# A planned kernel whose planner holds late work out of the opening and counts transposes behind a full wire as longer

## The chip, the cores and the metric

The kernel runs on one core of one Trainium2 chip. The metric is the device time of one execution in microseconds (us).

Engines are named as in the profile: PE is the tensor engine, PEld its weight loads, DVE the vector engine, ACT the scalar engine, POOL the GpSimd engine, SP the queue that issues the loads and the transposes. PSUM is the memory that the matmul results are written to, in banks; PE sometimes waits until ACT or DVE has taken a bank's content out.

## The reference, cut to what matters

A transformer block on 2048 tokens of width 1024: a layer norm, linear attention with 32 heads, an output product with a residual, a second layer norm and a gated ReLU block.

```python
qkv = _layernorm(x) @ wqkv                       # 2048 x 1024 @ 1024 x 3072
phi = lambda t: where(t > 0, t + 1, exp(t)) + 1e-6
kv  = einsum("bhsd,bhse->bhde", phi(k), v)       # summed over all tokens, so queries come last
o   = phi(q) kv / (phi(q) z + 1e-6)
h   = x + o @ wo
# ... layer norm of h, then relu(h @ W_gate) * (h @ W_up) @ W_down, plus h
```

Keys and values of all tokens are computed first, in eight pairs of 128-token tiles (pair p is tiles p and p + 8). Queries follow, after about 110 us.

Of the kernel before, what the change touches and what calls it, by code (L numbers as in the profile page):

```python
# [32 lines left out]
class Plan:  # L33
# [5 lines left out]
    SEM = 100.0  # L39
    WINDOW = 6000.0  # L40
    AHEAD = 120000.0

    class Node:
        __slots__ = ("eng", "calls", "preds", "hold", "lat", "open", "dma", "late", "ready", "left", "start", "nom")
# [155 lines left out]
    def schedule(self):  # L200
        nodes = self.nodes
        succs = self.order()
        engines = ("tensor", "vector", "scalar", "gpsimd", "sync")
        avail = {e: [] for e in engines}
        clock = {e: 0.0 for e in engines}
        for i, v in enumerate(nodes):
            v.left, v.ready = len(v.preds), max(0.0, v.late - self.AHEAD) if v.dma else 0.0
            if not v.left:
                avail[v.eng].append(i)
        pe = [i for i, v in enumerate(nodes) if v.eng == "tensor"]  # L210
        done, first, wire, out = set(), 0, 0.0, []
        while True:
            best = None
            for e in engines:
                a = avail[e]
                if not a:
                    continue
                if e == "sync":
                    for i in a:
                        v = nodes[i]  # L220
                        if v.late - max(clock[e], v.ready) > 6000.0:
                            v.ready = max(v.ready, wire - 2000.0)
                if e == "tensor":
                    while first < len(pe) and pe[first] in done:
                        first += 1
                    limit = nodes[pe[first]].nom + self.WINDOW
                    a = [i for i in a if nodes[i].nom <= limit]
                    if not a:
                        continue
                s = max(clock[e], min(nodes[i].ready for i in a))  # L230
                if best is None or s < best[0]:
                    best = (s, e, a)
            if best is None:
                break
            s, e, a = best
            now = [i for i in a if nodes[i].ready <= s]
            i = min(now, key=lambda i: (nodes[i].nom if e == "tensor" else nodes[i].late, i))
            v = nodes[i]
            if e != "tensor":

                soon = [j for j in a if s < nodes[j].ready < s + 0.5 * v.hold and nodes[j].late < v.late - 1500.0]
                if soon:
                    i = min(soon, key=lambda j: (nodes[j].late, j))
                    v = nodes[i]
                    s = v.ready
            v.start = s
            clock[e] = s + v.hold
            end = s + v.hold + v.lat
            if v.dma:
                wire = max(wire, s + v.hold) + v.dma  # L250
                end = wire + v.lat - v.dma + min(4000.0, max(0.0, 0.25 * (v.late - s)))
            avail[e].remove(i)
            done.add(i)
            out.append(i)
            for j in succs[i]:
                w = nodes[j]
                r = clock[e] if w.eng == e else end
                w.ready = max(w.ready, r)
                w.left -= 1
                if not w.left:  # L260
                    avail[w.eng].append(j)
        assert len(out) == len(nodes)
        self.span = max(clock.values())
        return out
# [1283 lines left out]
```

## The kernel before: the parts that the change touches

The kernel does not issue its instructions as it meets them. A planner records every operation as a node, gives each a deadline by going backwards from the tensor engine's work, and then simulates the five engines with a cost table. On each engine it takes, among the nodes that are ready, the one due first (with small exceptions). Its variable `wire` is the time at which it expects the DMA engines to have moved everything issued so far.

```python
def order(self):
    # ... t runs over PE's work in program order: v.nom is its nominal start
    for i in range(n - 1, -1, -1):
        v = nodes[i]
        late = min((nodes[s].late for s in succs[i]), default=t + 1e4)
        v.late = late - v.hold - v.lat           # the deadline
        # ...

def schedule(self):
    # ...
    for i, v in enumerate(nodes):
        v.left, v.ready = len(v.preds), max(0.0, v.late - self.AHEAD) if v.dma else 0.0
        # ...
    # ... the main loop has picked node i of engine e, to start at s
            clock[e] = s + v.hold
            end = s + v.hold + v.lat
            if v.dma:                            # a load or store; a transpose has v.dma == 0
                wire = max(wire, s + v.hold) + v.dma
                end = wire + v.lat - v.dma + min(4000.0, max(0.0, 0.25 * (v.late - s)))
            # ... successors become ready at `end`
```

The products use a seven-product (Strassen-like) scheme, called a quad. Its left operands include four sums and differences of blocks of the normalised, transposed tokens, made on DVE. Each 128x512 sum takes some 0.4 us.

A token tile is normalised on POOL, in `finish`, and then transposed by a DMA from SBUF to SBUF:

```python
def finish(self):
    self.rstd_()                                 # two small ACT steps
    nc.gpsimd.tensor_scalar(out=xn, in0=self.x, scalar1=self.negm[:], scalar2=self.rstd[:],
                            op0=ALU.add, op1=ALU.mult)
    nc.sync.dma_start_transpose(out=XI[self.i][:, :, self.r:self.r + P], in_=xn)
    # ...
```

## Time and profile before

| | before |
|---|---|
| time, median of 3 runs | 727.32 us (727.05 to 729.67) |
| span of the profiled execution | 727.0 us |
| PE busy | 716.1 us, 98% |
| PE idle in the first 27 us | 1.18 + 0.55 + 0.68 + 2.02 us |
| DVE busy from 50 to 60 us | 8.12 of 10 us |

PE is the bound: it is busy nearly all the time, so the time can move only by its few pauses and by the clock. The lines that carry this are in the prediction. Two stretches of DVE that the prediction did not show turn out to matter. The first is the opening, in the profile of the kernel before (order of time; start us, length us, engine, line, operation, output<-input, count, and in brackets the idle time ahead of it with what ended it):

```profile
15.37 1.40 DVE L121 TENSOR_TENSOR mem<-mem 128x512 f16<-128x512 bf16 x3
...
29.39 0.66 DVE L121 TENSOR_TENSOR mem<-mem 128x512 f16<-128x512 bf16 x1
```

These four 128x512 sums, three and one, are those of pair 0. They run where DVE has pauses. The second stretch is the fifth pair's preparation, same view and kernel:

```profile
53.36 1.24 DVE L121 TENSOR_TENSOR mem<-mem 128x512 f16<-128x512 bf16 x3 [0.30 <-DMA mem<-mem]
...
55.12 0.41 DVE L121 TENSOR_TENSOR mem<-mem 128x512 f16<-128x512 bf16 x1
55.45 1.28 DVE L121 BATCH_NORM_STATS2 tiny<-mem 128x6 f32<-128x512 bf16 x2
...
57.45 0.29 DVE L121 TENSOR_SCALAR mem<-mem 128x512 bf16<-128x512 bf16 x1 [0.47 <-ACT mem L121]
57.68 0.58 ACT L121 COPY mem<-psum 128x512 f32<-128x512 f32 x1
```

Here DVE makes pair 4's four sums, then the statistics of a later tile. Its idle time in this stretch is 0.30 + 0.47 = 0.77 us. ACT takes the statistics' result in two small steps and then, at 57.68, copies a bank out of PSUM, which lets PE go on. PE does not pause.

### The profile page before, as it was taken

The page shows a single profiled execution, that of the slowest core. Times are in us where ns is not written, and L with a number is a line of the kernel's source. Part 1 is how long each engine was busy: PE and PEld are TensorE (multiplying, and loading weights), DVE is VectorE, ACT ScalarE, POOL GpSimd, SP SyncE. Part 2 cuts the span into 40 slices and gives each one's busy share as a digit, 9 for nine tenths or more (in the row PEclk, how much of TensorE's full clock was granted, in tenths as well). Part 3 has the DMA queues.
Part 4 walks back from the last instruction along what each step waited for, and adds up shares of the span by engine and source line. Part 5 has one row for each costly group of instructions (what it writes and reads, how often), then busy time and mean ns, then how long its engine had stood idle before and what let it go on. Part 6 is the DMA issues. An engine that isn't in the chain of part 4 may idle for free.

```text
span 727.0 us, 11233 instructions
## 1 busy us (share of the span) xinstructions
PE 716.1 (98%) x4163; PEld 397.3 (55%) x4163; DVE 562.2 (77%) x949; ACT 279.5 (38%) x544; POOL 78.7 (11%) x90
## 2 busy tenths in 40 slices
PE   8899999999999999999999999999999999999998
PEld 3354545444444444444444444444444688888887
DVE  6787755896897785575767968759668878999996
ACT  5688545666555443323333333333333220001100
POOL 2343000002202120000000000000000004101452
PEclk9999999999999999999999999999999999999999
DMA  9465605239775730456156485685582878777974
GB/s 304 107 139 117 159 1 167 67 79 225 158 162 146 145 87 0 120 150 180 51 152 190 148 250 165 189 254 180 160 287 72 265 263 203 223 274 232 243 84 60
DMA packets 156503, 117.40 MB, mean 161 GB/s; under 512 B 54944, under 2 KB 140192, under 8 KB 156320
## 3 DMA queue, kind: packets, MB, share of 16 engines
q1 hardware_dynamic: 148832, 113.01, 54.5%
q0 software_dynamic: 7616, 3.67, 4.8%
q8 instruction: 32, 0.52, 0.3%
q14 instruction: 23, 0.19, 0.1%
HBM read 70.52 MB, written 34.08 MB: 144 GB/s over the span
## 4 chain that ended last, share of the span: by engine, by line
PE 90%; DVE 3%; ACT 3%; DMA 2%; issue 1%; POOL 0%; ACTq 0%; DVEq 0%
PE psum L121 90%; DVE mem L121 3%; ACT mem L121 2%; DMA mem<-mem 2%; DVE tiny L121 1%; POOL mem L121 0%; DMA mem<-in_A_x_dram 0%; ACT tiny L121 0%; ACTq L121 0%; DVEq L121 0%
## 5 line engine op out<-in xcount | busy, mean ns | idle before, releaser
L121 PE MATMUL psum<-mem 128*128 128x512 f16 (+4 forms) x4147 | 715.2, 335 | 6.9 <-DVE mem L121 2.6
L121 PEld LDWEIGHTS <-mem 128*128 128x128 f16 (+1 forms) x4163 | 397.3, 98 | 325.9 <-issue 8.2
L121 DVE TENSOR_TENSOR mem<-psum,mem 128x512 f32<-128x512 f32 (+2 forms) x240 | 187.2, 792 | 100.0 <-ACT mem L121 65.7
L121 DVE TENSOR_TENSOR mem<-mem 128x512 f16<-128x512 bf16 (+8 forms) x400 | 241.4, 642 | 18.3 <-DMA mem<-mem 11.0
L121 ACT COPY mem<-psum 128x512 f32<-128x512 f32 (+2 forms) x124 | 92.7, 749 | 211.8 <-PE psum L121 207.8
L121 ACT COPY psum<-psum 128x512 f32<-128x512 f32 (+1 forms) x68 | 49.1, 722 | 161.1 <-PE psum L121 157.1
L121 POOL DMA_DIRECT2D out_dram<-mem x28 | 34.1, 1302 | 413.8 <-DVE mem L121 413.7
L121 POOL TENSOR_SCALAR mem<-mem,tiny 128x1024 bf16<-128x1024 bf16 x30 | 39.1, 1305 | 200.3 <-ACT tiny L121 176.8
L121 ACT ACTIVATE mem<-psum 128x512 bf16<-128x512 f32 x90 | 53.8, 598 | 17.3 <-PE psum L121 16.8
L121 DVE SCALAR_TENSOR_TENSOR mem<-mem 128x512 bf16<-128x512 bf16 (+1 forms) x71 | 57.6, 812 | 1.3
L121 DVE SCALAR_TENSOR_TENSOR mem<-psum,mem 128x512 bf16<-128x512 f32 x66 | 45.4, 688 | 12.0 <-PE psum L121 7.9
L121 ACT ACTIVATE mem<-mem,tiny 128x1024 bf16<-128x1024 bf16 x25 | 28.6, 1144 | 10.6 <-DVE tiny L121 5.8
L121 DVE TENSOR_SCALAR mem<-mem 128x512 bf16<-128x512 bf16 (+1 forms) x49 | 16.7, 341 | 19.2 <-ACT mem L121 18.9
L121 ACT ACTIVATE mem<-mem 128x1024 bf16<-128x1024 f32 (+1 forms) x24 | 25.3, 1056 | 6.5 <-DVE mem L121 6.5
L121 DVE TENSOR_TENSOR mem<-psum,tiny 128x384 bf16<-128x384 f32 (+1 forms) x48 | 22.9, 507 | 5.3 <-ACT tiny L121 3.9
L121 ACT ACTIVATE tiny<-tiny 128x1 f32<-128x1 f32 (+2 forms) x112 | 22.6, 206 | 7.9 <-DVE tiny L121 5.0
L121 ACT ACTIVATE tiny<-psum 128x12 f32<-128x12 f32 (+1 forms) x48 | 8.1, 169 | 13.8 <-PE psum L121 13.4
L121 ACT CAST mem<-psum 128x512 bf16<-128x512 f32 x18 | 10.4, 580 | 2.6 <-PE psum L121 2.0
L121 DVE BATCH_NORM_STATS2 tiny<-mem 128x6 f32<-128x512 bf16 x14 | 9.1, 678 | 2.5 <-DMA mem<-in_A_x_dram 2.5
L121 POOL TENSOR_SCALAR tiny<-tiny 128x1 f32<-128x1 f32 x14 | 4.0, 288 | 23.6 <-ACT mem L121 18.4
L121 ACT ACTIVATION_READ_ACCUMULATOR mem<-mem,tiny 128x1 f32 x25 | 4.7, 189 | 0.0
L121 DVE TENSOR_SCALAR tiny<-tiny 128x1 f32<-128x1 f32 x16 | 3.3, 209 | 0.3
(18 smaller groups left out, 13.5 us busy)
## 6 DMA issues: line engine op xcount, KB each, us to landing
l_dram<-mem SPq DMA_DIRECT2D x98, 128.0 KB, 2.2
mem<-l_dram SPq DMA_DIRECT2D x12, 896.0 KB, 6.5
mem<-in_A_x_dram SPq DMA_DIRECT2D x32, 256.0 KB, 3.1
mem<-in_B_W_up_dram SPq DMA_DIRECT2D x14, 512.0 KB, 5.3
mem<-in_B_W_gate_dram SPq DMA_DIRECT2D x14, 512.0 KB, 4.5
mem<-in_B_W_down_dram SPq DMA_DIRECT2D x28, 256.0 KB, 3.7
r_dram<-mem SPq DMA_DIRECT2D x56, 128.0 KB, 2.0
mem<-r_dram SPq DMA_DIRECT2D x8, 896.0 KB, 6.1
```

What stands on the lines that cost most here:

```text
L121: call = lambda: getattr(getattr(self.nc, eng), op)(*args, **k)
```

## The change

The intent is to keep work that is due much later out of the opening stretch, where every engine has urgent work, and to have the planner count a transpose as later when the loads ahead of it fill the wire, so that PE's order doesn't rely on a landing that is too early. Its description also speaks of first loads in the order of their deadlines; that is no edit of its own: the whole diff is this.

```diff
@@ class Plan
     AHEAD = 120000.0
+    OPENING = 45000.0
@@ schedule, before the loop
             v.left, v.ready = len(v.preds), max(0.0, v.late - self.AHEAD) if v.dma else 0.0
+            if v.eng != "tensor" and v.late > 2.0 * self.OPENING:
+
+                v.ready = max(v.ready, self.OPENING)
@@ schedule, the planned landing
             if v.dma:
                 wire = max(wire, s + v.hold) + v.dma
                 end = wire + v.lat - v.dma + min(4000.0, max(0.0, 0.25 * (v.late - s)))
+            elif e == "sync":
+
+                end = max(end, min(wire + 800.0, end + 2500.0))
```

The first part is called the hold below, the second the landing rule.

## The prediction

> **What bounds the kernel now.** I read the page's head first, then the PE waits, the stretches, the chain of waits, and the issuing queue's order of time in the opening. The head says the tensor engine is the bound almost everywhere:
>
> ```profile
> PE 716.1 (98%) x4163; PEld 397.3 (55%) x4163; DVE 562.2 (77%) x949; ACT 279.5 (38%) x544; POOL 78.7 (11%) x90
> PE 90%; DVE 3%; ACT 3%; DMA 2%; issue 1%; POOL 0%; ACTq 0%; DVEq 0%
> ```
>
> PE is busy for 716.1 of 727.0 us, and 90% of the chain that ended last is PE. No change of order can give back more than the remaining 10.9 us, plus matmuls that ran at a reduced clock. So I ask where those us lie. The PE order of time has idle pieces of 1.18 us (before the first matmul), 0.55, 0.68 and 2.02 us in the first 27 us, then only 0.78 (at 152.7), 1.31 (at 194.2) and 0.55 us (at 204.8), and 3.5 us after the last matmul. The four of the opening make 4.4 us, and the 2.02 us one is the longest that PE has. Around it, the stretches (columns: PE, PEld, DVE, ACT, POOL busy with counts, PE clock, DMA share, GB/s):
>
> ```profile
> 24.00:25.00 1.00, 0.26 (x2) 0.00 (x0) 0.00 (x0) 0.97 (x4) 0.00 (x0) 1.00 0.08 16
> 25.00:26.00 1.00, 0.00 (x0) 0.00 (x0) 0.62 (x2) 0.62 (x2) 0.21 (x1) 1.00 0.02 8
> 26.00:27.00 1.00, 0.71 (x3) 0.31 (x4) 1.00 (x4) 0.00 (x0) 0.00 (x0) 0.91 0.00 0
> 27.00:28.00 1.00, 1.00 (x4) 0.39 (x3) 1.00 (x2) 0.27 (x1) 0.00 (x0) 0.50 0.00 0
> 28.00:29.00 1.00, 1.00 (x4) 0.36 (x3) 1.00 (x3) 1.00 (x4) 0.42 (x1) 0.50 0.00 0
> 29.00:30.00 1.00, 1.00 (x3) 0.30 (x2) 0.97 (x3) 1.00 (x2) 1.00 (x2) 0.50 0.00 0
> 30.00:31.00 1.00, 1.00 (x5) 0.45 (x4) 0.04 (x1) 0.26 (x2) 0.11 (x1) 0.88 0.01 2
> ```
>
> PE stands from 24.27 to 26.29 us, and then its granted clock is 0.91, 0.50, 0.50, 0.50, 0.88: the sum of what is missing is 0.09 + 0.50 + 0.50 + 0.50 + 0.12 = 1.71 us of full-speed time. The gap thus costs 2.02 + 1.7 = 3.7 us, not 2.0. The shorter gaps (0.68, 0.78, 1.31 us) are followed by no such dip. The chain of waits says what ended it:
>
> ```profile
> 18.41 1.81 POOL mem L121
> 20.22 0.02 issue
> 20.24 5.08 DMA mem<-mem
> 25.32 0.02 issue
> 25.34 0.43 DVE mem L121
> 25.78 0.02 issue
> 25.80 0.44 DVE mem L121
> 26.24 0.05 issue
> 26.29 33.10 PE psum L121 x168
> ```
>
> The normalised second token tile of pair 1 (tile 9) leaves POOL at 20.2 us, its DMA transpose takes 5.08 us from issue to landing, two DVE sums follow, and only then can the sixth product of the first key quad run. On the issuing queue the transpose stands behind bulk loads:
>
> ```profile
> 5.92 4.79 SPq L121 DMA_DIRECT2D mem<-in_A_wqkv_dram  x4
> 10.83 2.33 SPq L121 DMA_DIRECT2D mem<-in_A_x_dram  x2
> 17.98 1.35 SPq L121 DMA_TRANSPOSE mem<-mem  x1
> 19.43 0.52 SPq L121 DMA_DIRECT2D mem<-in_A_x_dram  x1
> 20.24 1.24 SPq L121 DMA_TRANSPOSE mem<-mem  x1
> ```
>
> From 5 to 20 us the stretches show DMA shares of 1.06, 1.09 and 0.96 at 353, 358 and 300 GB/s: a full wire. The median transpose lands 3.2 us after issue, this one after 5.08; the plan counts 1.25 + 2.35 = 3.6 us for each, whatever the wire carries.
>
> **What the Trainium skill says.** "TensorE: Matmul & The Clock Gate", Part 1, states that the PE clock falls to half after an idle window of about 3.4 us and comes back after some 3.4 us of sustained work, the window being free-running. The trace agrees on the half (0.50) and on the length of the dip (about 26.9 to 30.8 us), but here a gap of 2.02 us was enough; a window that also held other pauses might explain that, which no view shows. "DMA: Bandwidth & Descriptors", Issuing engines are not separate DMA queues, states that all DMAs share the same 16 engines and interleave; the transpose that takes 5.08 us beside loads, against 3.2 at the median, fits. The first page's Engine queue depths paragraph says that ACT and DVE are strict FIFO and that PE pulls only weight loads ahead. So an order planned on a landing that is too early is paid in full: PE stands at the sixth product although others could run.
>
> **The change part by part.** No operand, tile or instruction is added or removed: the same 11,233 instructions, in another planned order per engine. So the direct cost is zero, and only idle time can move.
>
> Part one holds everything but PE work that is due after 90 us until 45 us of plan time. I worked out by hand whom that touches, from the code's deadline rule, with 213 ns per 512-wide matmul (the traced full-speed rate: 60 in 13.12 us is 219). The prologue on PE ends at 14.7 us, one token pair takes 56 x 0.213 + 1.6 = 13.5 us, pair 1 has 3.4 us more, so pair 7 starts at 14.7 + 3.4 + 6 x 13.5 = 99 us. Everything for pairs up to 6 is due before about 86 us. Of pair 7 the transposes and the last steps of its normalisation are due at 91 to 96, but the trace issues the last transposes at 70 and 72 us, because the token buffers (four tiles) come free only as earlier tiles are normalised. The query weights are due later still, but they are already chained behind the last transpose (issued at 73.8 us); output weights, gate and up weights (from 117 us) need memory that key and value work occupies. In the first 45 us I find no executed instruction that the hold would move. I expect this part to be **nearly a null**: 0 us, with a small chance that I missed one load.
>
> Part two gives a transpose a later planned landing: the wire's planned end plus 0.8 us, at most 2.5 us more than now. It binds only where the planned backlog at issue exceeds 3.6 - 0.8 = 2.8 us. Before tile 9's transpose the plan has 14 loads of 5.5 MB and one tile load, which at the plan's 300 GB/s end near 20.6 us; a transpose issued at 18.5 to 20 would be counted to 22.1 to 23.6 already, and the new rule gives 21.4. By my hand it binds for tile 1's transpose (planned perhaps 1 to 2 us earlier, right behind the weight loads) and just misses for tile 9's; I trust this only to about 1 us, so I give 45% that tile 9's is lengthened or that its dependants move with tile 1's. Later, backlog occurs beside the gate and up loads around 199 to 204 us, and after out stores with tile loads from 150 to 190 us; PE idles there for only 0.78 + 1.31 + 0.55 = 2.6 us in all.
>
> If it binds, PE's planner sees the sixth product come later and takes what is ready within its 6 us window: the second product of the same quad (4 x 0.213 = 0.85 us; the bank copy it needs ended near 23.2) and perhaps the first product of the value quad (0.85 us). That fills 0.85 to 1.7 us of 2.02. A rest of 0.3 to 1.2 us is in the range of gaps that were followed by no clock dip, so the 1.7 us goes too: **a gain of 2.5 to 3.4 us**. If it does not bind, the gap stays, and other orders shift by tenths.
>
> **The rivals.** *Everything is hidden or null*: the gap's end is set by the real landing at 25.32 us and the two sums, and the path to that (ACT without a pause from 10.5 to 17.96 us, then POOL) isn't shortened by planning. For it: neither part speeds the transpose itself. Against it: PE had other ready work. Time 726.5 to 728. *A new wait*: work put ahead occupies DVE or a bank, so that the sums start after the landing, or a product goes early and its eviction delays the next quad. DVE stood for 1.54 us before the landing, so it has room; but ACT is 4.2 to 4.5 of 5 us busy from 10 to 25 us. Cost perhaps 1 to 2 us: 728 to 729. *Gains elsewhere too*: the three gaps from 150 to 205 us each hang on a transpose (3.11 and 4.82 us to landing) and could shrink by 1 to 2 us: 722 to 724 together with the opening. *Another engine as bound* I rule out: after 206 us PE has no gap until the end, and the change doesn't reach there in any way that a trace shows.
>
> **Range and chances.** Weights: opening gap mostly filled, about -3 us, 45%; null within 0.7 us, 35%; extra gain elsewhere, -4 to -5, 8%; worse by 1 to 2, 12%. Mean: 0.45 x (-3) + 0.08 x (-4.5) + 0.12 x 1.5 = -1.5; since the null and the filled gap are both likely I take -2.0 from 727.3, that is 725.3 us. The runs before spread from 727.05 to 729.67, so the upper end is 728.3; the lower end, the filled gap plus 1 us elsewhere, 722.0. Two per cent is 14.5 us, more than all idle time of PE; a loss of that size would need a stall in every stage. Faster 0.01, same 0.98, slower 0.01.
>
> **What would show it.** Right: the PE idle at 24.3 us is under 1.2 us, the granted clock stays near 1.00 from 26 to 31 us, bf16 products stand ahead of the first fp16 one there, and the 250 to 700 us stretch is as before. The null: the same 2.0 us gap and dip. Part one shown wrong: loads or normalisation steps that moved from before 45 us to after. The prediction fails if the free-running clock window drops at a shorter gap, or at another place, or if the new order delays the tile loads so that a later pair waits.

## More of the kernel before

```python
def left_sums(lo, n):
    # ... columns lo..lo+n of the four blocks a11, a12, a21, a22
    return [tt(s1, a21, a22, ALU.add), tt(s2, s1, a11, ALU.subtract),
            tt(s4, a12, s2, ALU.subtract), tt(s3, a11, a21, ALU.subtract)]

# ... pair 0: its keys and values are plain products, without sums
for p in range(1, NP):                           # NP = 8
    pk, kq = k_quad(p)
    # ...
    qs.run(kq)
    v, vq = v_quad(p)
    ls = left_sums((p + 1) % NP * P, P)          # at p = 7 this wraps to pair 0
    # ... queued behind the quads
```

Note the wrap. Pair 0 needs no sums for its keys and values, but the query quads read all columns, so its four sums are recorded at p = 7. Their inputs are ready as soon as pair 0 is transposed, at about 11 us.

## The result, and the profile after

| | before | changed |
|---|---|---|
| median of 6 runs | 727.98 us (726.82 to 729.75) | 730.54 us (729.18 to 731.99) |
| ratio | | 1.0033, 95% interval 1.001 to 1.0055 |
| span of the profiled execution | 727.0 us | 729.1 us |
| PE busy | 716.1 us | 716.1 us |
| DVE busy from 50 to 60 us | 8.12 us | 9.79 us |

The changed kernel is 0.33% slower: a small loss, but a resolved one, and a second series gave 1.0036 (1.0021 to 1.0051). A ratio is the mean time of one kernel's fast runs over that of the other's in the same rounds, so it is not quite the ratio of the medians quoted. Executions over 1.5% slower than the fastest of the same kernel are left out of the means. All outputs are right.

First, PE. Its busy time is the same to a tenth of a us, so all of the loss is idle time. The order of time of the changed kernel's PE:

```profile
26.99 32.01 PE L122 MATMUL psum<-mem 128*128 128x512 f16 x164 [2.47 <-DVE mem L122]
60.45 94.37 PE L122 MATMUL psum<-mem 128*128 128x512 f16 x518 [1.46 <-ACT mem L122]
155.60 40.71 PE L122 MATMUL psum<-mem 128*128 128x512 bf16 x219 [0.78 <-DMA mem<-mem]
```

The same view of the kernel before:

```profile
26.29 126.41 PE L121 MATMUL psum<-mem 128*128 128x512 f16 x682 [2.02 <-DVE mem L121]
153.47 40.70 PE L121 MATMUL psum<-mem 128*128 128x512 bf16 x219 [0.78 <-DMA mem<-mem]
```

Two things happened. The opening's pause ends 26.99 - 26.29 = 0.70 us later, and there is a **new pause of 1.46 us at 59 us**, where the kernel before ran on. Together that is 2.16 us. The next pause starts a piece at 155.60 against 153.47, 2.13 us later, so nothing else was lost or won on the way. After 75 us the chains of waits of the two kernels differ by a constant shift of 2.13 to 2.15 us.

Second, the opening. The stretches of the changed kernel (PE, PEld, DVE, ACT, POOL busy with counts, PE clock, DMA share, GB/s) show the same pause and the same dip of the clock, of the same size:

```profile
26.00:27.00 1.00, 0.01 (x1) 0.01 (x1) 0.91 (x3) 0.00 (x0) 0.18 (x1) 0.79 0.32 121
27.00:28.00 1.00, 1.00 (x3) 0.42 (x4) 1.00 (x3) 0.00 (x0) 0.00 (x0) 0.50 0.00 0
```

The clock column reads 0.79 and 0.50 here and 0.50 in the next two, so 0.21 + 3 x 0.50 = 1.71 us of full-speed time are missing.

Its chain of waits (start us, us, what) has a landing that is faster, 4.29 us against 5.08, but the transpose left later, at 21.73 us against 20.24:

```profile
21.73 4.29 DMA mem<-mem
...
26.99 16.75 PE psum L122 x82
```

(The two sums of DVE stand in between, as before.) So 1.49 us later at issue, 0.79 us given back on the wire, 0.70 us left. Where the 1.49 us came from is on POOL, which normalises the two tiles of pair 1 (tiles 1 and 9). POOL in the order of time, the kernel before, tile 1 and tile 9:

```profile
16.36 1.59 POOL L121 TENSOR_SCALAR mem<-mem,tiny 128x1024 bf16<-128x1024 bf16 x1
18.41 1.80 POOL L121 TENSOR_SCALAR mem<-mem,tiny 128x1024 bf16<-128x1024 bf16 x1 [0.46 <-POOL mem L121]
```

and the changed kernel:

```profile
17.31 1.20 POOL L122 TENSOR_SCALAR mem<-mem,tiny 128x1024 bf16<-128x1024 bf16 x1
19.39 2.32 POOL L122 TENSOR_SCALAR mem<-mem,tiny 128x1024 bf16<-128x1024 bf16 x1 [0.87 <-ACT tiny L122]
```

The first step starts 0.95 us later and is 0.39 us shorter, the pause between them is 0.41 us longer, and the second step takes 0.52 us more: 0.95 - 0.39 + 0.41 + 0.52 = 1.49. The late start has an origin further up, a small POOL step that ACT waits for, first the kernel before, then the changed one:

```profile
13.20 0.23 POOL L121 TENSOR_SCALAR tiny<-tiny 128x1 f32<-128x1 f32 x1 [10.75 <-ACT mem L121]
13.32 1.17 POOL L122 TENSOR_SCALAR tiny<-tiny 128x1 f32<-128x1 f32 x1 [10.86 <-ACT mem L122]
```

This part doesn't always repeat: of the runs with the same opening order, x_hold80 shows it (1.14 us), x_after2 and x_hold80b don't (0.25 and 0.23). What repeats is the distance from tile 1's transpose to tile 9's, shown under x_after2.

The second step's length is explained by DVE. The Trainium skill ("SBUF — State Buffer", SBUF: two separate sides) says that DVE and GpSimd share one pair of ports, that a DVE operation with two SBUF inputs takes it as an exclusive lock for the whole instruction against a GpSimd operation that reads SBUF, and that whoever comes second waits. The two DVE weight sums in question, before and changed:

```profile
17.61 1.41 DVE L121 TENSOR_TENSOR mem<-mem 128x2048 f16<-128x2048 bf16 x1
19.30 1.22 DVE L122 TENSOR_TENSOR mem<-mem 128x2048 f16<-128x2048 bf16 x1
```

These traces agree to 0.01 us: in the changed kernel DVE starts a weight sum with two inputs at 19.30 and holds it for 1.22 us, then POOL needs its own 1.20 us, and 19.30 + 1.22 + 1.20 = 21.72, where the step ended at 21.71. In the kernel before the sum began at 17.61 for 1.41 us: 17.61 + 1.41 + 1.20 = 20.22, ended 20.21.

Third, the new pause. The changed kernel from 53 us, all engines in the order of time:

```profile
53.41 3.08 DVE L122 TENSOR_TENSOR mem<-mem 128x512 f16<-128x512 bf16 x7
...
56.55 1.20 POOL L122 TENSOR_SCALAR mem<-mem,tiny 128x1024 bf16<-128x1024 bf16 x1 [2.25 <-issue]
57.01 1.01 DVE L122 TENSOR_TENSOR mem<-mem 128x512 f16<-128x512 bf16 x1
...
57.94 1.27 DVE L122 BATCH_NORM_STATS2 tiny<-mem 128x6 f32<-128x512 bf16 x2
...
59.49 0.44 ACT L122 ACTIVATE tiny<-tiny 128x1 f32<-128x1 f32 x2 [1.59 <-DVE tiny L122]
...
59.84 0.57 ACT L122 COPY mem<-psum 128x512 f32<-128x512 f32 x1
```

Where three sums stood there are now seven. The four additional ones take 3.08 - 1.24 = 1.84 us. They push the pair's last sum onto a POOL step, which holds the ports, so it takes 1.01 us in place of 0.41, another 0.60. (In this trace, x_move45 and x_act that sum starts 0.46, 0.54 and 0.59 us after the POOL step and ends 0.27, 0.28 and 0.28 us after the step's end: it waits for that end.) The statistics start 57.94 - 55.45 = 2.49 us later than before, ACT stands 1.59 us for them in its queue, its copy of the bank comes 59.84 - 57.68 = 2.16 us later, and PE waits for that copy: 0.70 us of the lag is the opening's, 1.46 us is new. By durations: 1.84 + 0.60 us of additional work less the 0.77 us in which DVE had stood idle is 1.67 us, of which PE shows 1.46; it had some 0.2 us of slack here. This is a balance of DVE's time and not the path itself, since 0.47 of the 0.77 us lie behind the statistics. On the path, counted from DVE's operation just before this stretch (at 52.38 us, and 52.81 in the changed kernel), the statistics start after 5.13 us in place of 3.07, 2.06 more. ACT's copy starts after 7.03 in place of 5.30, 1.73 more, and PE stands for 1.46 of that.

Which instructions moved is not a guess. The planned orders of the two kernels, which building them gives, were compared on every engine. PE, ACT, POOL and SP have the same order. On DVE this is all that moved (cut to what matters; - is before, + is changed; the first lines re-sort the opening's weight sums by a place):

```
 TensorTensor      mem<-mem 128x2048
+TensorScalarPtr   mem<-mem 128x512
+TensorScalarPtr   mem<-psum,mem 128x512
+TensorTensor      mem<-mem 128x2048
 TensorScalarPtr   mem<-mem 128x512
 TensorScalarPtr   mem<-psum,mem 128x512
-TensorTensor      mem<-mem 128x2048
-TensorScalarPtr   mem<-mem 128x512
-TensorScalarPtr   mem<-psum,mem 128x512
-TensorTensor      mem<-mem 128x4x128 x3
 ...
-TensorTensor      mem<-mem 128x4x128
 ...
-TensorTensor      mem<-mem 128x4x128 x3
+TensorTensor      mem<-mem 128x4x128 x7
```

Building the parts alone settles the authorship without any chip time. The landing rule alone gives the same order as before on all five engines: its condition held for none of the 46 transposes. For tile 1 the planned landing was 21.58 us against a wire end plus 0.8 us of 20.52; for tile 9, 23.35 against 21.40. The hold alone gives the changed kernel's order. And holding just pair 0's four sums gives it too: the plan has them due at 112 to 120 us, over the limit of 90, and starts them at 15.3 to 28.4 us, and no other operation outside PE is both due after 90 us and started before 45. **The change is four 0.4 us vector operations in another place.**

### The profile page after: what moved, and what is told of

Read it like the earlier page. It is cut to its first block, busy times and chain, and to the rows that moved or that the text cites. A ratio compares the mean times of both kernels' runs of the same rounds, so it can differ in the third digit from the quotient of the medians.

```text
span 729.1 us, 11231 instructions
## 1 busy us (share of the span) xinstructions
PE 716.1 (98%) x4163; PEld 397.2 (54%) x4163; DVE 563.6 (77%) x949; ACT 280.0 (38%) x544; POOL 79.8 (11%) x90
## 4 chain that ended last, share of the span: by engine, by line
PE 88%; DVE 5%; ACT 3%; DMA 2%; issue 1%; POOL 0%; ACTq 0%; DVEq 0%
PE psum L122 88%; DVE mem L122 4%; ACT mem L122 3%; DMA mem<-mem 2%; DVE tiny L122 1%; ACT tiny L122 0%; DMA mem<-in_A_x_dram 0%; POOL mem L122 0%; POOL tiny L122 0%; ACTq L122 0%; DVEq L122 0%
## 5 line engine op out<-in xcount | busy, mean ns | idle before, releaser
L122 DVE TENSOR_SCALAR mem<-mem 128x512 bf16<-128x512 bf16 (+1 forms) x49 | 17.5, 356 | 21.4 <-ACT mem L122 21.2
```

The lines of the kernel that those rows point to most:

```text
L122: call = lambda: getattr(getattr(self.nc, eng), op)(*args, **k)
```

## The experiments

The theory: the loss is the four sums' landing in a stretch where DVE has no room (about 1.5 us), plus a smaller loss of about 0.7 us because their absence from the opening re-times it. Rivals: (a) the landing rule does something after all; (b) the loss is only the opening's, with more frequent clock dips; (c) the pause at 59 us is a matter of ACT's order, not of DVE's load.

| run | what it is | median, us (before) | ratio (95%) | PE resumes | pause near 59 us |
|---|---|---|---|---|---|
| x_turn | landing rule alone | 728.14 (727.63) | 1.0005 (0.998 to 1.0029) | 26.56 | none |
| x_hold80 | four sums held to 80 us | 728.47 (727.63) | 1.0006 (0.9984 to 1.0027) | 27.23 | none |
| x_move45 | order of before, four sums moved to the busy place | 729.05 (727.63) | 1.0024 (1.0003 to 1.0045) | 26.36 | 1.45 |
| x_move80 | order of before, four sums moved behind 80 us | 729.45 (727.63) | 1.0016 (0.9995 to 1.0037) | 26.96 | none |
| x_move2 | as x_move45, two of the four sums | 727.58 (729.31) | 0.9988 (0.9969 to 1.0007) | 25.69 | none |
| x_act | x_move45 with one swap on ACT | 729.85 (729.31) | 1.0007 (0.999 to 1.0025) | 27.41 | 1.15 |
| x_dve19 | before, tiles 1 and 9 normalised on DVE | 729.2 (729.31) | 1.0003 (0.9989 to 1.0017) | 21.27 | see text |
| x_long | before, early transposes planned longer, always | 726.57 (729.31) | 0.9969 (0.9955 to 0.9983) | 25.44 | none |
| x_after2 | the changed kernel again | 730.92 (728.29) | 1.0036 (1.0021 to 1.0051) | 26.86 | 1.45 |
| x_hold80b | x_hold80 again | 728.34 (728.29) | 1.0003 (0.9986 to 1.002) | 26.79 | none |
| x_long_hold80 | x_long and four sums held to 80 us | 726.39 (728.29) | 0.9977 (0.9964 to 0.9991) | 25.44 | none |
| x_before2 | the kernel before, one look | 726.84 | | 25.75 | none |

The medians in brackets are those of the kernel before in the same rounds, on the same chip. They differ by 1.7 us from batch to batch, which is why only the ratios are compared. (The first four rows are one batch on one chip, the others two batches on another.) "None" means that the view, which merges the shortest pauses, shows no pause there.

### x_turn: the landing rule alone

```diff
             if v.dma:
                 ...
+            end = max(end, min(wire + 800.0, end + 2500.0)) if e == "sync" and not v.dma else end
```

> Only the second part (transposes planned longer). The built program has every engine's instructions in the same order as before. Both theories, and the theory that the second part matters, differ only here: mine expects a ratio of 1.000 +- 0.002 and the same trace (PE gap of 2.0 us at 24.3 us, no gap at 59 us); if the second part carried the loss, 1.003.

Measured: 1.0005 and no pause at 59 us. PE resumed at 26.56 us, within the scatter of the kernel before. Rival (a) falls: the rule is inert. An unplanned find came with it. The profiled execution had a pause of 2.34 us in the opening, longer than the 2.02 of the kernel before, and its clock stayed at 1.00 throughout.

### x_hold80 and its repeat x_hold80b: the sums held past the busy stretch

```diff
-            v.left, v.ready = len(v.preds), max(0.0, v.late - self.AHEAD) if v.dma else 0.0
+            v.left, v.ready = len(v.preds), max(max(0.0, v.late - self.AHEAD) if v.dma else 0.0,
+                                                80000.0 if i in self.early else 0.0)
@@ left_sums: remember the four nodes
+            ... nc.early.append(nc.last()) if (lo, n) == (0, P) ...
```

> Only the four sums of token pair 0 are held, and to 80 us of plan time instead of 45; the opening has the changed kernel's vector order. Theory A (two separate losses: 0.70 us from the reordered opening, 1.46 us from the four sums standing in the busy stretch at 45 to 60 us): PE resumes at 27.0 us as in the changed kernel, the 1.46 us gap at 59 us is gone, span +0.7 us over before. Rival B (one loss: the late opening alone pushes the later gap): both gaps stay, +2.1 us. Rival C (the sums alone): +0.

> A repeat of the sums held to 80 us, same opening order as the changed kernel. If the opening's reorder costs its 0.7 us by itself: 0.7 us over before in undipped spans; if the 0.7 us of the first two profiles was scatter of one execution: within 0.4 us of before. The small GpSimd step at 13.3 us takes about 1.15 us instead of 0.23 in either case.

Measured: 1.0006 and 1.0003. The opening is the changed kernel's, in the planned order and in the trace; the pause at 59 us is gone. PE in the order of time, x_hold80:

```profile
27.23 124.97 PE L121 MATMUL psum<-mem 128*128 128x512 f16 x682 [2.82 <-DVE mem L121]
```

One unbroken piece to 152.2 us, as in the kernel before. What follows: about 1.5 us of the loss belongs to the place where the sums come down, not to their leaving the opening. What is left, 0.2 to 0.4 us in the times with intervals of more than ±1 us, neither confirms nor excludes the opening's 0.7. The repeat was to decide by its executions without a clock dip (split below): their median span is 726.3 us, the same as that of the kernel before in the same rounds, which by the line drawn beforehand (0.4 us) speaks for scatter; the means differ by 0.5 us, so it stays open. The GpSimd step of 1.15 us that was expected in either case did not come: it took 0.23.

### x_move45: only the place, nothing else

Here the planner runs as before, and four entries are taken out of its finished order and put ahead of pair 4's sums.

```diff
-        for i in self.schedule():
+        out = self.schedule()
+        early = [i for i in out if i in self.early]
+        rest = [i for i in out if i not in self.early]
+        k = next(k for k, i in enumerate(rest) if self.nodes[i].eng == "vector" and self.nodes[i].start >= 50600.0)
+        for i in rest[:k] + early + rest[k:]:
```

> The order of before in the opening, the four sums only taken out of it and put where the changed kernel has them (before the sums of pair 4). Theory A: PE resumes at about 26.3 us as before, the gap near 59 us appears with 1.5 us (perhaps up to 0.7 us less or more as the opening ends earlier), span +1.4 us over before. Rival B: no gap near 59 us, +0. Rival C: +2.1 us.

```profile
58.40 21.49 PE L121 MATMUL psum<-mem 128*128 128x512 f16 x120 [1.45 <-ACT mem L121]
```

Measured: 1.0024 (1.0003 to 1.0045), and the pause is back at 1.45 us, with the opening otherwise as before. The sum of extra work can be redone on this trace: the group of seven took 3.20 us, 1.96 more, and the last sum 0.93, 0.52 more, together 2.48. Less DVE's 0.77 us of idle time that is 1.71, of which PE shows 1.45, so that its slack here was 0.26 us. Split by the clock dip (below), its five executions without one have a median span of 727.2 us against 725.8 for the nine of the kernel before in the same rounds, the 1.4 us expected. Moving these four operations alone, into this place, makes the pause.

### x_move80: the sums moved out of both places

The edit is that of x_move45 with 80000.0 for 50600.0.

> The order of before, the four sums taken out of the opening and put behind 80 us of plan time. Theory A: neither loss, span within 0.3 us of before; if the 1.4 us of vector work that leaves the opening had been on the path, up to 1 us less. Rivals B and C: also about +0. A check that the move by itself costs nothing when it goes to a quiet stretch.

Measured: 1.0016 (0.9995 to 1.0037); no pause at 59 us, 0.22 us at 80 us (x_move45, without the sums there, has 0.25, so that need not be their doing). Four of its six executions had the clock dip, so the ratio says little. Like for like, these four have a median span of 727.85 us and the other two 725.7, against 727.75 and 725.9 for the kernel before: no loss.

### x_move2: half the dose

The edit is that of x_move45, for the third and fourth sum only.

> Half the dose: of the four sums of pair 0, the first two stay in the opening, the last two (0.88 us of vector work) stand before the sums of pair 4. If the vector engine's queue is what limits from 46 to 59 us, with the slack that the full dose shows (1.76 us of sums gave a PE gap of 1.45 us, so 0.3 us slack), the gap near 58 us is 0.5 to 0.6 us and the undipped span about 0.6 us over before. If a threshold is at work (any late sums block), it stays 1.4 us; if not the vector queue, 0.

Measured: no pause near 58 us. I had expected 0.5 to 0.6 us, a miss. DVE in the order of time, x_move2, shows why:

```profile
50.67 2.29 DVE L121 TENSOR_TENSOR mem<-mem 128x512 f16<-128x512 bf16 x5
...
53.48 0.42 DVE L121 TENSOR_TENSOR mem<-mem 128x512 f16<-128x512 bf16 x1
```

Two sums add 2.29 - 1.24 = 1.05 us, and the pair's last sum, 0.42 us at 53.48, is not delayed, because it is nearly done when the POOL step starts, at 53.84. Less DVE's idle 0.77 us, 0.28 us is left, about what PE took as slack in the two traces before (0.21 and 0.26): nothing remains that the view would show. On the path the statistics start 0.67 us more behind that DVE operation than in the kernel before, and ACT's copy 0.34, where the full dose had 2.10 and 1.76 (x_move45). So the dose is not linear. The first two of the four sums fit in the slack; the other two pay in full and meet the port lock as well. My expectation had halved the full loss and left both terms out.

### x_act: is it ACT's order?

ACT stands 1.59 us for the statistics with the copy of the bank behind it in its queue. If that is the cause, putting the copy ahead of tile 6's two small steps should remove the pause. The edit is x_move45 and this swap, with whatever depends on the two steps.

> As the run with all four sums moved to 45 us, and one swap on the scalar engine: the snapshot that PE waits for goes ahead of the two small steps of tile 6's normalisation, which wait for the late vector statistics. If PE loses by way of the scalar queue's order: the gap near 58 us falls from 1.45 to under 0.3 us, and what is lost moves to at most 0.5 us elsewhere. If PE waits for the vector engine itself (banks freed late): the gap stays at 1 us or more, ended by the vector engine.

```profile
61.64 93.24 PE L121 MATMUL psum<-mem 128*128 128x512 bf16 x505 [1.15 <-DVE mem L121]
```

Measured: a pause of 1.15 us, a little later, and now ended by DVE in place of ACT. My theory of a blocked ACT queue, rival (c), falls as the cause: the swap took only 0.30 us off the pause. ACT was only the first place where DVE's backlog reached PE; take that away, and the next product that waits for DVE shows it.

### x_dve19: the port lock taken out of the opening

```diff
-                nc.gpsimd.tensor_scalar(out=xn, in0=self.x, ...)
+                (nc.vector if self.t in (1, 9) else nc.gpsimd).tensor_scalar(out=xn, in0=self.x, ...)
@@ neg: the negated mean of these two tiles on ACT
+                nc.scalar.activation(out=self.negm[:], in_=src, func=ACT.Copy, scale=by)  # tiles 1, 9
```

> Before, with the opening's path shortened: tiles 1 and 9 are normalised on the vector engine instead of GpSimd (0.55 us instead of 1.6 to 2.3), and their negated means made on the scalar engine. If the path scalar, GpSimd, transpose, sums sets the end of the 2.0 us gap, PE resumes 1.0 to 1.8 us sooner (24.6 to 25.3 us) and the undipped span falls by as much; if the wire sets the landing (transposes queue behind loads that are issued anyway), the transposes only take longer and PE resumes at about 26 us.

Measured: 1.0003 (0.9989 to 1.0017). The long pause became 1.41 us and moved to 19.86 to 21.27 us, but new pauses came at 31.00 (0.79), 44.50 (0.31), 53.72 (0.36) and 71.43 (0.21), each of them ended by ACT. The early gain was given back there; whether ACT or the DVE ahead of it is to blame, this run can't tell. None of its six executions had the clock dip, and that hides a loss in the ratio: their median span is 727.4 us against 726.1 for the four executions of the kernel before without a dip in these rounds, where a gain of as much as the earlier landing had been expected.

### x_long: the landing rule as it was meant

The landing rule never binds, so the idea behind it was still untested. Here it binds by force:

```diff
+            end += 1800.0 if e == 'sync' and not v.dma and s < 25000.0 else 0.0
```

> Before, with the planned landing of transposes issued in the first 25 us put 1.8 us later without a condition, so that the plan does see tile 9's transpose late (the second part of the change as it was meant). As my prediction argued: PE takes one or two products of 0.85 us ahead of the sixth, the gap of 2.0 us falls to 0.3 to 1.2 us, span 1 to 2 us less (more if the clock dip goes too). Rival: the order doesn't change on PE or the products put ahead delay their followers; gap as before, span within 0.5 us.

```profile
25.44 51.87 PE L121 MATMUL psum<-mem 128*128 128x512 f16 x278 [0.98 <-DVE mem L121]
```

Measured: **0.9969 (0.9955 to 0.9983)**, faster than the kernel before. PE's order changed: the fifth product of the first key quad, which needs only the first of the two sums, and the value quad's first product now stand ahead of the sixth. So PE resumes one sum earlier, after 0.98 us in place of 2.02. In no execution did the clock dip. The executions without a dip have a median span of 724.8 us against 725.9 for the kernel before, a gain of 1.1 us; and 7 of the 11 executions of the kernel before in these rounds had the dip, at about 1.7 us each.

### x_long_hold80: both cures together

The edits of x_long and x_hold80 together.

> Candidate that beats both: transposes of the first 25 us planned 1.8 us longer without a condition, and the four sums held to 80 us. If the two add up: as the longer plan alone (0.997), perhaps 0.3 us better or worse; no clock dip in most runs, PE gap near 25 us about 1 us, no gap near 59 us.

Measured: 0.9977 (0.9964 to 0.9991), PE resuming at 25.44 us again, after 1.11 us, and again without a dip in any of six executions. Both versions beat the kernel before and, by their ratios to it, the changed one. From each other they are not told apart.

### x_after2 and x_before2: how much the opening varies

> The changed kernel once more, beside the next two in the same rounds. If the loss is the sums in the busy stretch (1.5 us) and the opening's reorder costs little: ratio 1.002 to 1.004, gap of 1.4 to 1.5 us near 59 us again, and 1.5 to 2 us above the run with the sums held to 80 us.

> The kernel before, one more look at its trace. How far the opening scatters by itself: PE should resume between 25.7 and 27 us, with or without the dip of the granted clock to 0.5 behind it.

The changed kernel has the pause near 59 us again, 1.45 us, and a ratio of 1.0036. Its median is 2.6 us above x_hold80b's, more than the 1.5 to 2 expected; five of its six executions had the clock dip and one of x_hold80b's six, which is worth some 1.1 us of it. The opening varies from execution to execution of the same program: in x_before2 the kernel before had two pauses there, of 0.65 and 0.69 us, in place of the one of 2.02. With the order of before PE resumed at 26.29, 26.56 and 25.75 us (mean 26.20); with the changed opening at 26.99, 27.23, 26.86 and 26.79 (mean 26.97). That is 0.77 us, with no overlap, but over seven executions only. Taking just the sums out of the order of before gave 26.36, 26.96 and 27.41. One thing held in all thirteen traces that normalise on POOL: from the issue of tile 1's transpose to that of tile 9's it was 2.26 to 2.27 us in the five that have the first two sums in the opening, and 3.18 to 3.19 us in the eight that have all four out of it. Tile 1's own transpose left at 17.98 to 19.08 us with the order of before and at 18.41 to 18.54 with the changed opening, so it is tile 9's that the change delays. Without the sums, the weight sum and tile 9's normalisation start together and the latter waits for the whole of it.

### The clock dip

The executions of the kernel before in the three later batches, and those of the changed kernel in both of its series, can be split by their mean granted clock into those with the dip (0.998 or less) and those without. For the kernel before: 20 without, median span 725.9 us, and 12 with, 727.75 us. For the changed kernel: 4 without, 727.7 us, and 8 with, 729.25 us. The five traces with the dip (before, changed, x_move80, x_act, x_after2) each miss 1.70 to 1.71 us of full-speed time in the clock column, and no other trace misses any there. So the dip costs some 1.7 us whatever the kernel, and **the change costs 1.8 or 1.5 us like for like**. The changed kernel had the dip more often, 8 of 12 against 12 of 32. If that were a real difference it would add (0.67 - 0.38) x 1.7 = 0.5 us; so few executions don't show that it is. Rival (b), that dips explain the loss, is at most this part.

## Why the prediction was wrong

The prediction was 725.3 us with a range of 722.0 to 728.3; the kernel took 730.54. The class, within 2%, was right; the direction, a gain of 2 us, was wrong.

**What bounds the kernel** was right. PE's busy time didn't change, the 2.02 us pause was a real place to gain, the stretch from 250 to 700 us is as before (so is everything after 75 us, but for the shift), and the only differences are idle time.

**Part one is the step that failed.** It said: "In the first 45 us I find no executed instruction that the hold would move", and "I expect this part to be nearly a null". I had gone through transposes, normalisation steps, query, output and gate weights, all by the deadlines of the pair that they belong to. The four sums that the value quad of pair 7 records are those of pair 0, due with the queries (112 to 120 us in the plan), and they run at 15 and 29 us. The wrap in `left_sums((p + 1) % NP * P, P)` was there to read. The term counted as 0 measured 1.46 us at 59 us (with 1.45 in x_after2 and x_move45), and about 0.7 us in the opening by the traces, which the times neither confirm nor exclude.

**Part two** had the right working and too generous a chance. The prediction's own number, a rule value of 21.4 us that "just misses for tile 9's", was exact: 21.40 against a planned 23.35. For tile 1 the hand's "it binds" was wrong: 20.52 against 21.58. The 45% for a filled pause rested on distrust of that number "to about 1 us", where the margins were 1.95 and 1.06 us. Building the rule alone showed that it binds nowhere, and x_turn showed no effect.

**The mechanism behind part two's gain was right**, though this change doesn't set it off. With the landing planned longer by force, PE's planner did put other products ahead of the sixth (the fifth and the value quad's first, where I had named the second and the value quad's first), the pause fell from 2.02 to 0.98 us, inside the "0.3 to 1.2 us" foreseen, the dip didn't come in any of twelve executions, and the time fell. The size, "a gain of 2.5 to 3.4 us", was somewhat too big: the ratio of 0.9969 is worth 0.0031 x 728 = 2.3 us. The dip that it avoids is not there in every execution of the kernel before, only in 12 of 32, where the prediction's 1.7 us counted it in full.

**The rivals.** "*A new wait*", with work "put ahead" that "occupies DVE or a bank", named the right engine and the right size, 1 to 2 us, at 12%. But it had work pulled forward in mind. What happened is that work put off landed on a later, fuller stretch. No rival asked where held work comes down. The range's upper end, 728.3, was built from a null with the scatter of the runs before; the kernel before ran at 727.98 beside the changed one, so that range had 0.3 us of room for a loss, and left out most of the 728 to 729 that the prediction gave to this very rival. "*Gains elsewhere too*" misread one of its three pauses: the last, 0.55 us at 204.8, is ended by DVE, and the chain of waits has no transpose between 195.5 us and it.

**The clock.** The prediction took 2.02 us as a pause that makes a dip and the shorter ones as pauses that don't. A single trace misled there. Other executions with 2.34 and 2.82 us had no dip. That PE pulls *only* weight loads ahead is the prediction's reading of its page, which says that PE can pull them; this agrees so far as PE stood 2.02 us in the planned order and 0.98 us in x_long, where ready products stood first.

What stays open: how much of the loss the opening has in the times. Traces say 0.7 to 0.8 us; x_hold80 and its repeat have +0.4 and +0.2 us with intervals that hold both zero and 0.8; split by the dip, their eight executions without it have a median span of 726.15 us against 725.9, and their three with it 727.3 against 727.75.

## What to carry to other kernels

Before work is held back "because it is due much later", find out which instructions that is, by comparing the planned orders, and look at the stretch into which they will come down: work that fills an engine's early idle time for nothing is better left there than moved to a stretch in which that engine has no room. Here past 80 us was, within the intervals, as good a place as the opening. A planner's rule with a condition needs a check that the condition ever holds; the same idea, once it bound, gained 0.3%. And where a pause ends at one engine's wait, changing the order in that engine's queue shows whether it is the cause or only the first to show another's backlog.

## What the Trainium skill lacked or had wrong

- "TensorE: Matmul & The Clock Gate", Part 1, puts the fall of the clock after an idle window of about 3.4 us. Here no pause before the last matmul was that long, and the clock fell to 0.50 around pauses of 2.02 and 2.47 us, while it stayed at 1.00 after 2.34 and 2.82 us in other executions. The page's remark that the window is free-running and that the effect varies from run to run fits (12 of 32 executions of one program had the dip); how short a pause can bring the fall is not said there, and 2.02 us was enough here.
- "DMA: Bandwidth & Descriptors", DMA Transpose (X-bar), gives constraints but no landing time (the page has an effective bandwidth for it in another table). On this core a 128x1024 transpose from SBUF to SBUF took 3.1 us from issue to landing where little else was under way (at 152.44 us in the changed kernel), and 4.29 and 5.08 us behind loads; the planner counted 3.6 us for all.
